# Reciprocals of three blocks repeated by transfers inside SBUF, keys' weight in one load, and a new order of the work

## The chip, the cores and the metric

The kernel runs on one core of a Trainium2 chip. The core has an engine for matrix products (TensorE, PE in the profile; its weight loads are listed apart as PEld), one for elementwise work on 128 lanes (VectorE, DVE), one for activation functions (ScalarE, ACT), one for general work (GpSimd, POOL) and a sequencer that issues transfers (SyncE, SP). Sixteen DMA engines carry these transfers. On-chip memory is SBUF (128 partitions) and PSUM (eight banks of 2 KB in each partition, written by PE and read by DVE and ACT). The engines run side by side, each through its own list of instructions in order, and wait for one another by semaphores.

The metric is the device time of one execution in microseconds (us).

## The reference

One layer over 2048 tokens of width 512, in bfloat16: linear attention with 32 heads of width 16, then a dense block with relu, each behind a layer norm and with a residual.

```python
h  = x + A(layernorm(x), wqkv, wo)
h2 = h + B(layernorm(h), w1, w2)

def A(x, wqkv, wo):
    q, k, v = heads(x @ wqkv)                   # 32 heads of 16
    phi = lambda t: where(t > 0, t + 1, exp(t)) + 1e-6
    pq, pk = phi(q), phi(k)
    kv  = einsum("bhsd,bhse->bhde", pk, v)      # one 16 x 16 matrix a head
    z   = einsum("bhsd->bhd", pk)
    num = einsum("bhqd,bhde->bhqe", pq, kv)
    den = einsum("bhqd,bhd->bhq", pq, z) + 1e-6 # one number a token and head
    return merge(num / den) @ wo

def B(x, w1, w2):                               # w1: 512 x 1792, w2: 1792 x 512
    return relu(x @ w1) @ w2
```

## The kernel before

Tokens are cut into 16 tiles of 128 and into 4 blocks of 512. Everything that is computed is a named step. The text `ORDER` at the head of the file lists the steps, with a tile or block, a part and a PSUM bank as numbers behind the name; a loop at the end of the file calls them one by one, and so fixes the order in which each engine, and SP's queue, meets its own instructions. An instruction that waits holds all that stand behind it on its engine. The blocks are numbered 0 to 3 in the order; "blocks 2 to 4" of the change are those with the numbers 1 to 3.

*Keys.* Loads of the input are `lx` (L212); weights come by `lk`, `lq`, `lv`, `lo`, `l1`, `l2` (L215; `lk.0.2` loads the first two of the four 128-row parts of the keys' weight). Statistics of a tile are `S` and `A` (L229, L230), the reciprocal deviation is `R` (L235, L236), the normalized tile is `N` (L243). Its transpose goes over PE (`T`, L262, evicted by `E` on ACT, L272, or `V` on DVE, L275) or over a transposing transfer on SP (`X`, L283). `K` is the product for the keys (L291); the feature map is `F` and `U` on ACT (L309, L312) and `M` and `D` on DVE (L316, L319). `G` adds each tile's product of normalized input and keys (L343) into four PSUM banks, `za` sums the keys on DVE (L351), `z` finishes the sum (L366). `gA` (ACT, L380) and `gD` (DVE, L383) evict G's banks in two halves, `kv` and `kx` (L388, L396) make the heads' matrices and `m` multiplies them by `wo` (L400), evicted by `mD` (L406) or `mA` (L403).

*Queries.* `Q` is the product for one 128-row part of a block's queries (L299), `qF`, `qU`, `qM`, `qD` its feature map on the same lines as the keys', two parts at once. `d4` forms the denominators of a block (L414), `dl4` and `dx4` take the logarithm and the exponential of its negative on ACT (L420, L425), so that `rd` holds 1/den: 8 heads for each of the four parts, in partitions 32j to 32j+7. To multiply the queries, each of these rows must stand in 16 partitions. For block 0 PE repeats them (`rp`, L430) and DVE multiplies out of PSUM (`rm`, L436). For blocks 1 to 3 `wb` (L442) writes `rd` to DRAM, and eight transfers `rb` (L445) read it back, each into 16 partitions of `rr` and all four parts; `dm` (L452) then multiplies two parts of the block on DVE. There is one `rr` for all blocks.

*Output of the attention and the dense block.* `h` is the product for one tile (L461), `hD` adds the residual on DVE (L467), `s` and `a` are the second statistics (L231, L232), `n` subtracts the mean (L250), `r` the reciprocal deviation; the transposes are `x` (SP, L284) or `t` (PE, L262, evicted by `v` on DVE, L281, or `e` on ACT, L278). `p` is the product with one 128-row part of `w1` for a block (L476), `ph` for half a block (L485); the relu goes out on ACT (`pA`, L491) or DVE (`pD`, L496), two parts at once. `f` is the product with `w2` for a tile, in two halves of seven parts (L505), `fo` scales and adds the residual (L513), `fd` stores (L520). The last tile's `f` is cut into three pieces by columns.

Of the kernel before, what the change touches and what calls it, by code (L numbers as in the profile page):

```python
# [15 lines left out]


ORDER = """
table const masks warm.70.7.64 warm.3.7 lx.1.1 S.1 lx.0.1 S.0 lx.3.1 lx.2.1 lx.4.2 A.1 S.3 A.0 R.1.1 R.0.1 S.2
A.3 N.1 A.2 N.0.0.2 N.0.2.2 S.5 R.2.2 T.0.0.0.2 T.0.3.2.2 T.1.1 warm.1.7 E.0.2.2 E.0.0.2 lk.0.2 lk.2.2 N.3  # L20
T.3.3 A.5 S.4 N.2 A.4 lx.6.2 K.0.0 T.2.2 E.1 K.1.1 R.4.2 V.3 F.0.1 U.0.1 F.1.1 U.1.1 V.2 K.2.2 N.4 T.4.0 F.2.1
E.4 M.0.1 N.5 lx.8.4 D.0.1 S.6 S.7 M.1.1 A.6 A.7 D.1.1 S.8 R.6.2 G.0 T.5.1 K.3.3 K.4.0 E.5 G.1 K.5.1 U.2.1
F.3.1 U.3.1 N.7 S.9 A.8 N.6 M.2.1 A.9 M.3.1 D.2.1 R.8.2 lx.12.4 X.7 X.6 F.4.2 U.4.2 G.2 D.3.1 N.8 S.13 N.9
A.13 M.4.2 S.12 D.4.2 A.12 R.12.2 G.3 K.7.3 K.6.2 X.8 X.9 lq.0.2 F.6.2 U.6.2 G.4 K.8.0 S.11 S.10 A.10 N.13
A.11 M.6.2 N.12 K.9.1 R.10.2 U.8.2 F.8.2 D.6.2 X.13 X.12 S.15 N.10 A.15 S.14 A.14 N.11 M.8.2 D.8.2 R.14.2 N.15
N.14 za.4 X.10 X.11 lq.2.2 X.15 X.14 lv.0.2 l1.2.2 lv.2.2 l2.7.7 lo.0.2 lo.2.2 l1.0.2 G.5 G.6 G.7 K.13.1
K.12.0 G.8 K.10.2 K.11.3 F.12.2 U.12.2 F.10.2 U.10.2 Q.0.0.0 Q.0.1.1 G.9 qU.0.0.2 M.12.2 za.6 M.10.2 D.12.2
D.10.2 za.8 za.10 K.14.2 K.15.3 G.10 G.11 G.12 G.13 F.14.2 U.14.2 qF.0.0.2 Q.0.2.0 M.14.2 za.12 D.14.2 G.14 zf
G.15 zhi zlo qM.0.0.2 qD.0.0.2 z.2.2 z.0.2 z.1.2 Q.0.3.1 z.3.2 zc gA.0.2 Q.1.1.3 Q.1.0.2 gD.2.2 qF.0.2.2
qU.0.2.2 qF.1.0.2 qU.1.0.2 kv.2.4 kv.1.4 kv.3.4 kv.0.4 qM.0.2.2 zh qD.0.2.2 qM.1.0.2 kx qD.1.0.2 Q.1.3.1  # L30
Q.1.2.0 qF.1.2.2 m.2.6 m.3.7 d4.0.3 m.0.4 m.1.5 mD.2.2 mD.0.2 Q.2.0.2 dl4.0 dx4.0 qU.1.2.2 Q.2.1.3 rp.0.3.7
# [7 lines left out]
s.4 a.4 s.7 a.5 n.4 a.7 p.0.13.3 p.0.12.2 r.0.4 pD.0.12.2 pA.0.10.2 d4.2.0.2 dl4.3 dx4.3 f.0.4.0.7 dl4.2 dx4.2
f.1.5.0.7 n.5 n.7 f.3.7.0.7 f.0.4.7.7 f.2.6.7.7 f.1.5.7.7 x.4 x.7 wb.2 x.5 x.6 p.1.1.1 p.1.0.0 rb.2.0 rb.2.4  # L40
rb.2.6 rb.2.1 wb.3 rb.2.5 fo.0 rb.2.7 rb.2.2 rb.2.3 p.1.2.2 p.1.3.3 pD.1.0.2 p.1.5.1 p.1.4.0 pA.1.4.2 r.4.4
pD.1.2.2 fo.2 dm.2.2.2 dm.2.0.2 f.3.7.7.7 p.1.8.0 p.1.6.2 h.10.6 hD.10 fo.1 fd.1 fo.3 rb.3.6 rb.3.2 rb.3.7
p.1.7.3 h.8.4 pA.1.6.2 p.1.9.1 h.11.7 hD.8 f.4.4.0.7 p.1.10.2 hD.11 s.10 s.11 a.11 n.11 pA.1.8.2 p.1.13.1
h.9.5 hD.9 s.9 a.9 f.7.7.0.7 p.1.11.3 a.10 s.8 rb.3.3 rb.3.0 rb.3.4 rb.3.1 rb.3.5 p.1.12.0 pA.1.10.2 pA.1.12.2
f.5.5.0.7 f.7.7.7.7 n.10 n.9 a.8 r.8.4 x.9 fd.2 dm.3.2.2 dm.3.0.2 n.8 fd.3 fd.0 fo.7 x.8 x.10 x.11 f.6.6.0.7
f.5.5.7.7 h.15.7 fo.5 f.6.6.7.7 p.2.0.0 h.13.5 p.2.1.1 f.4.4.7.7 p.2.2.2 fo.6 pA.2.0.2 p.2.4.0 h.14.6 p.2.3.3
pA.2.2.2 hD.15 hD.13 s.15 fo.4 p.2.5.1 h.12.4 p.2.7.3 pA.2.4.2 p.2.6.2 hD.14 s.13 p.2.8.0 p.2.9.1 hD.12 s.14
a.15 a.13 s.12 a.14 a.12 pD.2.6.2 r.12.4 n.15 pA.2.8.2 n.14 n.13 n.12 x.13 fd.7 fd.6 x.15 fd.5 x.14 x.12
f.11.7.0.7 f.10.6.0.7 f.9.5.0.7 p.2.12.0 p.2.11.3 p.2.10.2 p.2.13.1 pD.2.10.2 pA.2.12.2 f.8.4.0.7 f.9.5.7.7
p.3.0.0 p.3.1.1 f.10.6.7.7 pA.3.0.2 p.3.3.3 p.3.5.1 p.3.4.0 p.3.2.2 pA.3.4.2 f.8.4.7.7 p.3.9.1 pD.3.2.2  # L50
p.3.6.2 p.3.8.0 f.11.7.7.7 p.3.7.3 fo.11 pA.3.8.2 fo.9 fd.4 fo.10 fo.8 p.3.12.0 p.3.13.1 pD.3.12.2 fd.10 fd.9
pA.3.6.2 f.13.5.0.7 p.3.11.3 p.3.10.2 pD.3.10.2 f.12.4.0.7 f.15.7.0.14.0.2 f.12.4.7.7 fd.8 fd.11 f.14.6.0.7
f.13.5.7.7 fo.15.0.2 fo.12 fo.13 fd.12 fd.13 fd.15.0.2 f.14.6.7.7 fo.14 fd.14 f.15.5.0.14.3.1 fo.15.3.1
# [5 lines left out]
def kernel(  # L59
# [288 lines left out]
    def op_za(t):  # L350
# [205 lines left out]
```

## Time and profile before

| What | Value |
|---|---|
| Three runs | 170.84, 218.47, 170.45 us; median 170.84 |
| Span of the profiled execution | 169.2 us |
| Its time outside the span | not recorded; the two lower runs lie 1.25 and 1.64 us above the span |
| Busy: DVE, ACT | 101.0 us (60%), 65.4 us (39%) |
| Clock granted to PE | full in all of the 40 slices |
| DVE's wait for PE at the relu eviction (L496) | 26.7 us, in 6 waits |
| ACT's wait for PE at the relu eviction (L491) | 57.4 us, in 13 waits |
| Matmuls of 512 columns | 379 ns each on the page, 216 ns apart in a run of them |

The span runs from the first to the last instruction. The profile's durations of single matmuls overlap; what a run of them costs is read from the chain of waits, which follows the end of the program back, at each step to what released it. Idle time of DVE and ACT is mostly time in which they wait for PE.

### The profile page before, as it was taken

How to read it: one execution, taken by the hardware profiler on the slowest of the kernel's cores; microseconds unless marked ns; L12 is line 12 of the kernel's file. 1: busy time of each engine (PE TensorE's matmuls, PEld its weight loads, DVE VectorE, ACT ScalarE, POOL GpSimd, SP SyncE). 2: the span in 40 equal slices, each digit the busy share in tenths (PEclk: the TensorE clock that was granted, in tenths of full speed). 3: DMA queues.
4: the chain of work that ended last, by engine and by line, in shares of the span. 5: the costliest groups of instructions: out<-in, count | busy, mean ns of one | idle time of the engine just before them, and what ended most of it. 6: DMA issues, size and time to landing. Idle time of an engine off the chain costs nothing.

```text
span 169.2 us, 2376 instructions
## 1 busy us (share of the span) xinstructions
PE 163.5 (97%) x906; PEld 79.9 (47%) x922; DVE 101.0 (60%) x208; ACT 65.4 (39%) x96; POOL 4.7 (3%) x21
## 2 busy tenths in 40 slices
...
GB/s 135 279 210 50 111 119 153 281 364 259 1 2 4 62 133 208 0 4 59 104 147 2 18 94 48 155 62 0 0 0 97 124 31 0 0 0 127 1 31 93
DMA packets 23163, 15.10 MB, mean 89 GB/s; under 512 B 13808, under 2 KB 22128, under 8 KB 23152
## 3 DMA queue, kind: packets, MB, share of 16 engines
...
q8 instruction: 7, 0.11, 0.3%
...
## 4 chain that ended last, share of the span: by engine, by line
PE 91%; DMA 3%; SPq 1%; issue 1%; DVE 1%
PE bk L505 29%; PE bk L476 26%; PE bk L343 8%; PE bk L461 8%; PE bk L291 8%; PE bk L299 7%; DMA wk_sb<-in_A_wqkv_dram 3%; PE bk L485 2%; SPq L212 1%; PE bk L262 1%; DVE pqs L436 1%; PE bk L414 1%; PE bk L400 1%; PE bk L388 1%; PE bk L366 0%
## 5 line engine op out<-in xcount | busy, mean ns | idle before, releaser
L505 PE MATMUL bk<-w_sb,at 128*128 128x512 bf16 (+2 forms) x248 | 50.7, 355 | 0.2
L476 PE MATMUL bk<-lnT,w_sb 128*128 128x512 bf16 x203 | 47.9, 379 | 0.2
L491 ACT ACTIVATE at<-bk 128x1024 bf16<-128x1024 f32 x19 | 19.2, 1023 | 64.7 <-PE bk L476 57.4
L505 PEld LDWEIGHTS <-at 128*128 128x128 bf16 x252 | 23.5, 98 | 25.3 <-issue 0.4
L476 PEld LDWEIGHTS <-w_sb 128*128 128x128 bf16 x208 | 20.4, 98 | 24.3
L496 DVE TENSOR_SCALAR at<-bk 128x1024 bf16<-128x1024 f32 x9 | 11.0, 1219 | 26.7 <-PE bk L476 26.7
L513 DVE SCALAR_TENSOR_TENSOR gT<-bk,rstd,h_nat 128x512 bf16<-128x512 f32 (+2 forms) x18 | 12.1, 689 | 21.6 <-PE bk L505 19.2
L309 ACT ACTIVATE eb<-bk 128x1024 bf16<-128x1024 f32 (+1 forms) x18 | 16.6, 928 | 5.8 <-PE bk L291 4.3
L312 ACT ACTIVATE rb<-bk 128x1024 bf16<-128x1024 f32 (+1 forms) x18 | 16.4, 925 | 2.8 <-PE bk L299 2.4
L467 DVE TENSOR_TENSOR h_nat<-bk,x_nat 128x512 bf16<-128x512 f32 x16 | 10.9, 684 | 9.6 <-PE bk L461 9.5
L461 PE MATMUL bk<-m_sb,pqs 128*128 128x512 bf16 x63 | 15.9, 379 | 0.3 <-DVE pqs L436 0.2
L291 PE MATMUL bk<-wk_sb,lnT 128*128 128x512 bf16 x62 | 15.3, 379 | 0.2 <-DMA wk_sb<-in_A_wqkv_dram 0.2
L299 PE MATMUL bk<-lnT,wq_sb 128*128 128x512 bf16 x62 | 15.2, 379 | 0.1
L343 PE MATMUL bk<-at,h_nat 128*128 128x512 bf16 x55 | 13.2, 379 | 0.1
L229 DVE BATCH_NORM_STATS2 st<-x_nat 128x6 f32<-128x512 bf16 x16 | 10.6, 677 | 1.8 <-DMA x_nat<-in_A_x_dram 1.8
L231 DVE BATCH_NORM_STATS2 st<-h_nat 128x6 f32<-128x512 bf16 x16 | 10.6, 680 | 0.1
L461 PEld LDWEIGHTS <-pqs 128*128 128x128 bf16 x64 | 6.1, 98 | 8.0 <-DVE pqs L436 0.7
L343 PEld LDWEIGHTS <-h_nat 128*128 128x128 bf16 x64 | 6.2, 98 | 7.3
L291 PEld LDWEIGHTS <-lnT 128*128 128x128 bf16 x64 | 6.1, 98 | 7.4 <-issue 0.5
L299 PEld LDWEIGHTS <-wq_sb 128*128 128x128 bf16 x64 | 5.9, 98 | 6.6 <-issue 0.2
L316 DVE TENSOR_SCALAR eb<-eb 128x1024 bf16<-128x1024 bf16 (+1 forms) x18 | 6.8, 386 | 2.1 <-ACT eb L309 2.1
L235 ACT ACTIVATE rstd<-mv,eps 128x2 f32<-128x2 f32 (+2 forms) x13 | 3.8, 295 | 7.0 <-DVE mv L230 4.7
...
## 6 DMA issues: line engine op xcount, KB each, us to landing
...
out_dram<-gT SPq DMA_DIRECT2D x15, 128.0 KB, 1.9
rr<-scr SPq DMA_DIRECT2D x24, 64.0 KB, 2.7
...
x_nat<-in_A_x_dram SPq DMA_DIRECT2D x4, 128.0 KB, 2.2
...
```

The lines of the kernel that those rows point to most:

```text
L291: nc.tensor.matmul(bk[:, b, :], lhsT=lnT[c][:, kd, j * P : (j + 1) * P], rhs=wk_sb[:, kd, :], start=(kd == 0), stop=(kd == KD - 1),)
L299: nc.tensor.matmul(bk[:, b, :], lhsT=wq_sb[:, kd, j * P : (j + 1) * P], rhs=lnT[c][:, kd, :], start=(kd == 0), stop=(kd == KD - 1),)
L309: nc.scalar.activation(out=buf(eb, kind, i, n), in_=bank(at_bank[kind, i], n), func=ACT.Exp)
L312: nc.scalar.activation(out=buf(rb, kind, i, n), in_=bank(at_bank[kind, i], n), func=ACT.Relu)
L343: nc.tensor.matmul(bk[:, KD + kd, :], lhsT=ln_nat[:, t, kd * P : (kd + 1) * P], rhs=pk(t)[:, 0, :], start=(t == 0), stop=(t == NT - 1),)
L461: nc.tensor.matmul(bk[:, b, :], lhsT=pqs[:, (c * KD + jb) % NQ, j * P : (j + 1) * P], rhs=m_sb[:, jb, :], start=(jb == 0), stop=(jb == KD ...
L467: nc.vector.tensor_tensor(out=h_nat[:, t : t + n, :], in0=bank(at_bank["h", t], n), in1=x_nat[:, t : t + n, :], op=ALU.add,)
L476: nc.tensor.matmul(bk[:, b, :], lhsT=w1_sb[:, kd, f * P : (f + 1) * P], rhs=lnT[c][:, kd, :], start=(kd == 0), stop=(kd == KD - 1),)
L491: nc.scalar.activation(out=acts[c % 2][:, f : f + n, :], in_=bank(at_bank["p", c, f], n), func=ACT.Relu)
L496: nc.vector.tensor_scalar(out=acts[c % 2][:, f : f + n, :], in0=bank(at_bank["p", c, f], n), scalar1=0.0, scalar2=None, op0=ALU.max,)
L505: nc.tensor.matmul(bk[:, b, 0 : w * P], lhsT=acts[c % 2][:, f, j * P : (j + 1) * P], rhs=w2_sb[:, f, k * P : (k + w) * P], start=(f == 0), ...
L513: nc.vector.scalar_tensor_tensor(out=o_t[:, t % NO, cols], in0=bk[:, at_bank["f", t, k], 0 : w * P], scalar=rstd2[:, t : t + 1], in1=h_nat ...
```

## The change

The reciprocals of blocks 1 to 3 no longer go to DRAM. Four transfers `rs` for each block read the 8 rows of a part j straight out of `rd` in SBUF, each row 16 times, and write the 128 partitions of `rr[:, j, :]`. The keys' weight comes in one load of 512 KB, the queries' weight in one load of 512 KB ahead of the last loads of the input, and the four `Q` of block 0 stand among the first keys. `gA` becomes a `gD`, one `mD` an `mA`, one `V` an `E`, one `v` an `e`; four of the relu evictions go from ACT to DVE. `n` now gives the mean minus the value, so that the relu evictions multiply by -1. The bookkeeping of `G`, `za` and `z` allows any order of tiles. The whole order is new. The diff, with the order cut to the part around the reciprocals and the start:

```diff
 ORDER = """
-table const masks warm.70.7.64 warm.3.7 lx.1.1 S.1 lx.0.1 S.0 lx.3.1 lx.2.1 lx.4.2 A.1 S.3 A.0 R.1.1 R.0.1 S.2
-A.3 N.1 A.2 N.0.0.2 N.0.2.2 S.5 R.2.2 T.0.0.0.2 T.0.3.2.2 T.1.1 warm.1.7 E.0.2.2 E.0.0.2 lk.0.2 lk.2.2 N.3
...
-rp.0.0.4 rp.0.1.5 rp.0.2.6 Q.2.2.0 Q.2.3.1 qM.1.2.2 rm.0.0.2 rm.0.2.2 h.0.4 qD.1.2.2 hD.0 h.1.5 h.3.7 qU.2.0.2
-qU.2.2.2 qF.2.0.2 qF.2.2.2 d4.1.4 h.2.6 dl4.1 dx4.1 Q.3.2.0 Q.3.3.1 s.0 hD.1 a.0 hD.3 s.1 n.0 a.1 hD.2 n.1 s.3
-s.2 a.3 qU.3.2.2 qF.3.2.2 x.0 wb.1 rb.1.2 rb.1.4 rb.1.6 rb.1.0 rb.1.7 rb.1.5 rb.1.3 rb.1.1 l2.0.7 a.2 n.3
-Q.3.1.3 t.1.5 Q.3.0.2 n.2 v.1 t.3.7 t.2.6 v.3 v.2 ph.0.3.1.0 ph.0.2.0.0 ph.0.3.1.1 ph.0.2.0.1 qF.3.0.2
-qU.3.0.2 pA.0.2.2 ph.0.0.2.1 ph.0.0.2.0 ph.0.1.3.1 ph.0.1.3.0 p.0.6.0 p.0.7.1 pD.0.6.2 dm.1.0.2 dm.1.2.2
-qM.2.2.2 qM.2.0.2 pA.0.0.2 p.0.5.3 p.0.4.2 p.0.11.1 p.0.10.0 h.6.6 qM.3.0.2 pA.0.4.2 hD.6 h.4.4 h.5.5 p.0.9.3
...
+table const masks warm.70.7.64 warm.2.7 lx.0.1 S.0 lx.1.1 S.1 A.0 R.0.1 A.1 lx.3.1 lx.2.1 R.1.1 S.3 N.0.0.2 A.3
+R.3.1 T.0.1.0.2 N.0.2.2 T.0.3.2.2 E.0.0.2 N.1 T.1.1 N.3 E.0.2.2 S.2 lk.0.4 A.2 T.3.4 V.3 lx.4.2 E.1 K.0.5 K.1.2
+R.2.1 N.2 U.0.1 F.0.1 lx.6.2 T.2.7 E.2 K.3.1 S.4 S.5 A.4 M.0.1 F.1.1 K.2.4 A.5 S.7 lq.0.4 M.1.1 R.4.2 Q.0.1.3
+A.7 lx.12.4 F.3.1 N.4 N.5 M.3.1 S.6 D.0.1 lv.2.2 A.6 U.1.1 U.3.1 D.3.1 T.4.7 lx.8.4 lo.2.2 T.5.5 E.4 E.5 Q.0.2.0
+R.6.2 K.4.6 lv.0.2 K.5.7 Q.0.3.1 D.1.1 S.15 N.6 A.15 F.2.1 U.2.1 Q.0.0.2 F.4.2 S.13 N.7 A.13 U.4.2 S.9 S.14 A.9
+qF.0.0.2 qU.0.0.2 M.2.1 A.14 S.8 D.2.1 A.8 S.12 R.8.2 G.1 G.0 G.3 M.4.2 A.12 X.7 N.9 R.14.2 R.12.2 N.8 D.4.2
+N.13 X.6 X.9 S.10 S.11 qF.0.2.2 K.7.3 A.10 qM.0.2.2 K.6.2 G.4 G.2 G.5 F.6.2 U.6.2 A.11 R.10.2 N.12 N.14 qM.0.0.2
...
+K.14.2 F.14.2 U.14.2 M.14.2 G.8 zf D.14.2 G.11 G.10 G.13 zhi zlo qM.1.0.2 qD.1.0.2 G.15 z.2.2 G.14 G.12 gD.0.2
+gD.2.2 z.3.2 z.1.2 z.0.2 Q.1.3.1 Q.1.2.0 qF.1.2.2 kv.3.3 kv.2.3 kv.0.3 kv.1.3 zc zh d4.0.4 kx Q.2.0.2 m.2.5
+m.3.6 qU.1.2.2 qM.1.2.2 qD.1.2.2 m.1.1 dl4.0 m.0.0 dx4.0 mD.2.2 Q.2.1.3 rp.0.3.7 rp.0.0.4 mA.0.2 rp.0.2.6
+rp.0.1.5 Q.2.2.0 qU.2.0.2 qF.2.0.2 Q.2.3.1 qU.2.2.2 rm.0.0.2 rm.0.2.2 d4.1.5 qM.2.0.2 h.0.3 hD.0 s.0 h.1.4 dl4.1
+dx4.1 hD.1 rs.1.0 h.2.2 qF.2.2.2 Q.3.0.3 Q.3.1.4 h.3.0 Q.3.2.5 a.0 hD.2 n.0 s.1 s.2 a.1 qU.3.0.2 qF.3.0.2 a.2
+n.1 hD.3 x.0 rs.1.2 rs.1.3 t.1.2 e.1 n.2 rs.1.1 Q.3.3.6 s.3 a.3 qM.3.0.2 n.3 t.2.7 v.2 ph.0.2.0.0 ph.0.0.2.0
+t.3.4 l2.0.7 r.0.4 qM.2.2.2 ph.0.1.3.0 ph.0.3.1.0 v.3 ph.0.0.2.1 ph.0.1.3.1 ph.0.3.1.1 dm.1.2.2 qF.3.2.2
+ph.0.2.0.1 qU.3.2.2 pA.0.0.2 qM.3.2.2 dm.1.0.2 h.7.7 h.6.2 p.0.6.6 qD.2.2.2 qD.2.0.2 qD.3.0.2 qD.3.2.2 hD.7
+pD.0.2.2 hD.6 s.7 d4.2.4.2 dl4.2 s.6 dl4.3 h.5.3 p.0.7.7 a.7 pD.0.6.2 hD.5 a.6 dx4.2 p.0.10.0 h.4.2 hD.4 n.7
+rs.2.2 rs.2.1 rs.2.3 s.5 p.0.11.1 s.4 a.5 rs.2.0 dx4.3 n.6 p.0.9.5 p.0.4.6 p.0.5.7 x.7 p.0.13.3 p.0.8.4 p.0.12.2
+a.4 r.4.4 n.5 dm.2.0.2 n.4 pD.0.4.2 f.1.6.0.7 pD.0.10.2 dm.2.2.2 h.9.0 h.8.1 pD.0.8.2 h.11.5 x.5 pD.0.12.2 x.4
+rs.3.0 rs.3.1 dm.3.0.2 hD.8 f.1.6.7.7 hD.9 s.8 hD.11 a.8 h.10.7 s.9 x.6 p.1.7.2 p.1.6.1 rs.3.2 rs.3.3 dm.3.2.2
+a.9 hD.10 s.11 p.1.11.5 s.10 n.9 a.10 a.11 n.8 n.10 h.14.0 pA.1.6.2 h.12.2 n.11 hD.14 x.11 r.8.4 h.13.7 hD.12
...
+f.8.7.0.7 fo.14 fo.11 fd.11 fo.13 fd.13 fd.14 f.8.7.7.7 fo.8 fd.8 f.15.0.0.14.2.1 fo.15.2.1 fd.15.2.1
 """
...
     def op_n(t):
         nc.vector.tensor_scalar(
-            out=hn[:, t % NQ, :], in0=h_nat[:, t, :], scalar1=mv2[:, t, 0:1], scalar2=None,
-            op0=ALU.subtract,
+            out=hn[:, t % NQ, :], in0=h_nat[:, t, :], scalar1=-1.0, scalar2=mv2[:, t, 0:1],
+            op0=ALU.mult, op1=ALU.add,
         )
...
+    def op_rs(c, j):
+        rows = rd[j * Q4 : j * Q4 + P // DH, c, :]
+        nc.sync.dma_start(
+            out=rr[:, j, :], in_=rows.rearrange("h (o n) -> h o n", o=1).broadcast_to([P // DH, DH, CW])
+        )
...
     def op_pA(c, f, n):
         nc.scalar.activation(
-            out=acts[c % 2][:, f : f + n, :], in_=bank(at_bank["p", c, f], n), func=ACT.Relu
+            out=acts[c % 2][:, f : f + n, :], in_=bank(at_bank["p", c, f], n), func=ACT.Relu, scale=-1.0
         )
 
     def op_pD(c, f, n):
         nc.vector.tensor_scalar(
             out=acts[c % 2][:, f : f + n, :], in0=bank(at_bank["p", c, f], n),
-            scalar1=0.0, scalar2=None, op0=ALU.max,
+            scalar1=-1.0, scalar2=0.0, op0=ALU.mult, op1=ALU.max,
         )
```

More of the change, by code (lines that the diff above doesn't have):

```diff
@@ L24 @@
[L24 to L28, printed above, removed]
@@ L29 @@
-G.15 zhi zlo qM.0.0.2 qD.0.0.2 z.2.2 z.0.2 z.1.2 Q.0.3.1 z.3.2 zc gA.0.2 Q.1.1.3 Q.1.0.2 gD.2.2 qF.0.2.2
-qU.0.2.2 qF.1.0.2 qU.1.0.2 kv.2.4 kv.1.4 kv.3.4 kv.0.4 qM.0.2.2 zh qD.0.2.2 qM.1.0.2 kx qD.1.0.2 Q.1.3.1
-Q.1.2.0 qF.1.2.2 m.2.6 m.3.7 d4.0.3 m.0.4 m.1.5 mD.2.2 mD.0.2 Q.2.0.2 dl4.0 dx4.0 qU.1.2.2 Q.2.1.3 rp.0.3.7
-rp.0.0.4 rp.0.1.5 rp.0.2.6 Q.2.2.0 Q.2.3.1 qM.1.2.2 rm.0.0.2 rm.0.2.2 h.0.4 qD.1.2.2 hD.0 h.1.5 h.3.7 qU.2.0.2
-qU.2.2.2 qF.2.0.2 qF.2.2.2 d4.1.4 h.2.6 dl4.1 dx4.1 Q.3.2.0 Q.3.3.1 s.0 hD.1 a.0 hD.3 s.1 n.0 a.1 hD.2 n.1 s.3
@@ L34 @@
-s.2 a.3 qU.3.2.2 qF.3.2.2 x.0 wb.1 rb.1.2 rb.1.4 rb.1.6 rb.1.0 rb.1.7 rb.1.5 rb.1.3 rb.1.1 l2.0.7 a.2 n.3
-Q.3.1.3 t.1.5 Q.3.0.2 n.2 v.1 t.3.7 t.2.6 v.3 v.2 ph.0.3.1.0 ph.0.2.0.0 ph.0.3.1.1 ph.0.2.0.1 qF.3.0.2
-qU.3.0.2 pA.0.2.2 ph.0.0.2.1 ph.0.0.2.0 ph.0.1.3.1 ph.0.1.3.0 p.0.6.0 p.0.7.1 pD.0.6.2 dm.1.0.2 dm.1.2.2
-qM.2.2.2 qM.2.0.2 pA.0.0.2 p.0.5.3 p.0.4.2 p.0.11.1 p.0.10.0 h.6.6 qM.3.0.2 pA.0.4.2 hD.6 h.4.4 h.5.5 p.0.9.3
-h.7.7 p.0.8.2 pA.0.8.2 f.2.6.0.7 qD.3.0.2 qD.2.2.2 hD.5 qM.3.2.2 hD.4 s.6 qD.2.0.2 qD.3.2.2 a.6 n.6 hD.7 s.5
@@ L39 @@
[L39 to L53, printed above, removed]
@@ L54 @@
-fd.15.3.1 f.15.4.0.14.2.1 fo.15.2.1 fd.15.2.1
+table const masks warm.70.7.64 warm.2.7 lx.0.1 S.0 lx.1.1 S.1 A.0 R.0.1 A.1 lx.3.1 lx.2.1 R.1.1 S.3 N.0.0.2 A.3
[3 more added lines that the diff above has]
+R.6.2 K.4.6 lv.0.2 K.5.7 Q.0.3.1 D.1.1 S.15 N.6 A.15 F.2.1 U.2.1 Q.0.0.2 F.4.2 S.13 N.7 A.13 U.4.2 S.9 S.14 A.9
@@ new lines @@
+qF.0.0.2 qU.0.0.2 M.2.1 A.14 S.8 D.2.1 A.8 S.12 R.8.2 G.1 G.0 G.3 M.4.2 A.12 X.7 N.9 R.14.2 R.12.2 N.8 D.4.2
+N.13 X.6 X.9 S.10 S.11 qF.0.2.2 K.7.3 A.10 qM.0.2.2 K.6.2 G.4 G.2 G.5 F.6.2 U.6.2 A.11 R.10.2 N.12 N.14 qM.0.0.2
+K.9.3 N.11 M.6.2 qU.0.2.2 qD.0.0.2 D.6.2 N.15 X.8 K.8.2 X.13 K.13.1 X.12 F.8.2 U.8.2 G.6 N.10 K.12.0 F.12.2
+qD.0.2.2 M.8.2 X.11 K.11.3 za.4.1 X.10 D.8.2 za.6.0 M.12.2 G.7 U.12.2 za.8.0 K.10.2 F.10.2 M.10.2 X.15 X.14
+D.12.2 Q.1.1.1 U.10.2 D.10.2 lo.0.2 Q.1.0.0 qU.1.0.2 qF.1.0.2 l1.0.2 l1.2.2 za.10.0 za.12.0 G.9 l2.7.7 K.15.3
@@ new lines @@
+a.4 r.4.4 n.5 dm.2.0.2 n.4 pD.0.4.2 f.1.6.0.7 pD.0.10.2 dm.2.2.2 h.9.0 h.8.1 pD.0.8.2 h.11.5 x.5 pD.0.12.2 x.4
+rs.3.0 rs.3.1 dm.3.0.2 hD.8 f.1.6.7.7 hD.9 s.8 hD.11 a.8 h.10.7 s.9 x.6 p.1.7.2 p.1.6.1 rs.3.2 rs.3.3 dm.3.2.2
+a.9 hD.10 s.11 p.1.11.5 s.10 n.9 a.10 a.11 n.8 n.10 h.14.0 pA.1.6.2 h.12.2 n.11 hD.14 x.11 r.8.4 h.13.7 hD.12
+s.14 p.1.10.4 hD.13 h.15.3 a.14 s.12 x.9 p.1.2.1 x.8 pA.1.10.2 n.14 p.1.3.2 a.12 hD.15 s.13 n.12 a.13 s.15 x.12
+p.1.12.4 p.1.13.5 f.2.0.0.7 p.1.5.7 a.15 pA.1.2.2 r.12.4 n.13 n.15 fo.1 x.10 p.1.4.6 f.3.1.0.7 pA.1.12.2 p.2.0.2
@@ new lines @@
+pA.1.4.2 p.2.1.3 f.0.5.0.7 p.2.3.7 p.2.2.6 f.2.0.7.7 fo.2 pA.2.0.2 f.3.1.7.7 p.2.9.3 fo.3 p.2.8.2 pA.2.2.2
+f.0.5.7.7 fo.0 fd.2 pA.2.8.2 p.1.0.4 p.2.13.3 p.2.12.2 pA.2.12.2 p.2.11.7 p.2.10.6 x.15 p.1.1.5 pA.2.10.2
+pD.1.0.2 p.2.6.2 x.13 p.2.7.3 pD.2.6.2 p.1.8.4 p.1.9.5 x.14 pD.1.8.2 f.6.0.0.7 f.6.0.7.7 fo.6 f.4.7.0.7 fd.0
+f.4.7.7.7 fd.1 fo.4 f.5.3.0.7 fd.3 fd.4 fd.6 f.5.3.7.7 f.7.0.0.7 fo.5 f.7.0.7.7 fo.7 fd.7 p.3.8.6 p.3.9.7
+p.3.7.4 p.3.6.3 pA.3.8.2 p.3.0.6 p.3.1.7 pA.3.6.2 p.3.4.2 p.3.5.3 pA.3.0.2 pD.3.4.2 p.3.11.5 p.3.10.4 p.3.2.1
@@ L55 @@
+p.3.3.2 pD.3.10.2 p.3.13.7 p.3.12.6 pD.3.2.2 pA.3.12.2 f.15.5.0.14.0.2 fo.15.0.2 f.15.3.0.14.3.1 fo.15.3.1
+p.2.5.5 p.2.4.4 f.12.2.0.7 fd.5 fd.15.3.1 pD.2.4.2 f.12.2.7.7 fo.12 f.9.3.0.7 f.9.3.7.7 fo.9 f.10.5.0.7
+f.10.5.7.7 fo.10 f.14.0.0.7 f.14.0.7.7 f.11.5.0.7 f.11.5.7.7 f.13.1.0.7 fd.15.0.2 fd.10 fd.9 fd.12 f.13.1.7.7
+f.8.7.0.7 fo.14 fo.11 fd.11 fo.13 fd.13 fd.14 f.8.7.7.7 fo.8 fd.8 f.15.0.0.14.2.1 fo.15.2.1 fd.15.2.1
 """
@@ L87 @@
     NO = 4
-    ZT = 12
     const = ctx.enter_context(tc.tile_pool(name="const", bufs=1))
```

19 lines of the change are left out of this document (12 added, 7 removed).

## The prediction

> **What bounds the kernel now.** I read the page first. TensorE (PE) is busy for 163.5 of 169.2 us at a full granted clock, and the chain that ended last is 91% PE:
>
> ```profile
> span 169.2 us, 2376 instructions
> ...
> PE 163.5 (97%) x906; PEld 79.9 (47%) x922; DVE 101.0 (60%) x208; ACT 65.4 (39%) x96; POOL 4.7 (3%) x21
> ...
> PE 91%; DMA 3%; SPq 1%; issue 1%; DVE 1%
> ```
>
> Then the chain in order of time, to see where PE is not the bound:
>
> ```profile
> 3.61 4.93 DMA wk_sb<-in_A_wqkv_dram
> 8.54 0.04 issue
> 8.58 0.59 PE bk L291 x2
> ...
> 9.39 1.73 PE bk L291 x8
> ...
> 49.68 1.23 DVE pqs L436
> ...
> 58.70 3.49 PE bk L485 x32
> ...
> 75.80 0.55 PE bk L414 x8
> ```
>
> From 8.58 us to 166.53 us PE runs almost without a gap; the only other piece of note is the 1.2 us on VectorE (DVE) at 49.68. The matmul work of the new order is the same (only eight warm-up matmuls go). So a gain can come only from the 8.5 us ahead of the dense stretch, some 2.7 us behind it, and that one wait; a loss comes from every wait that the new order puts in front of PE. PE's prices are read here: four 512-column matmuls 0.86 us (eight in 1.73), four of 256 columns 0.44 (32 in 3.49), eight L414 0.55.
>
> **The reciprocals.** Twenty-four reads of 64 KB and three writes to DRAM go, twelve transfers of 128 KB come. The groups of DMA issues give the old prices, the timeline of the DMA queue (SP) when they ran:
>
> ```profile
> rr<-scr SPq DMA_DIRECT2D x24, 64.0 KB, 2.7
> ...
> scr<-rd SPq DMA_DIRECT2D x3, 128.0 KB, 1.9
> ```
>
> ```profile
> 56.56 0.53 SPq L442 DMA_DIRECT2D scr<-rd  x1
> 58.48 3.62 SPq L445 DMA_DIRECT2D rr<-scr  x8
> ```
>
> What goes saves nothing: asked for the tile `rr`, the trace names nobody who waited for it. DVE reached the multiply (L452) at 65.17 us, after the last issue at 61.7 had landed. SP loses about 5 us of issues (27 of 0.3 to 0.5 us for 12), and SP is not on the chain.
>
> What comes has no row: a transfer out of 8 partitions of `rd`, each read 16 times, into 128. Let r be the time for which one of them holds the queue. Below, the bound is SP's own pace, 0.42 us an issue (the median of L445). Above, the nearest row is the old `rr` transfer, the only one with few partitions (16, on the writing side). While eight of them ran, the windows show:
>
> ```profile
> 60.00:61.00 1.00, 1.00 (x12) 0.89 (x10) 0.00 (x0) 0.75 (x2) 0.00 (x0) 1.00 0.43 137
> ...
> 62.00:63.00 1.00, 0.95 (x6) 0.51 (x6) 0.00 (x0) 0.77 (x1) 0.00 (x0) 1.00 0.53 148
> ...
> 65.00:66.00 1.00, 1.00 (x7) 0.47 (x5) 1.00 (x3) 0.31 (x1) 0.00 (x0) 1.00 1.08 385
> ```
>
> The last column is GB/s: 137 for 16 partitions, 385 for a weight load over 128. At 137/16 = 8.6 GB/s a partition, 8 partitions carry 68 GB/s, and 128 KB take 1.9 us. I take 1.9, the nearest row in partitions touched, though those reads may have been held by the pace of issue. From issue to the first packet is 1.05 us (the first load: issued 0.80, first packet 1.83); from the last packet to landing 0.4 (`scr`: 58.06 to 58.46).
>
> **Block 2** (reciprocals index 1). Let T be the start of h.0. PE then has h.0, h.1, h.2, Q.3.0, Q.3.1, h.3, Q.3.2, Q.3.3 (8 x 0.86), three transposes (0.66) and eight half projections (8 x 0.44): h.7 is due at T+11.1. It needs all four parts of `rr` through dm.1.2 and dm.1.0. On DVE one start follows the last by 0.61 (L467), 0.60 (L231, L319, L452), 0.09 (L232), 0.27 (L250), 0.33 (L316), 1.14 (L496). n.0 is done at T+3.75 (h.2 ends at 2.6, 0.2 to its add, 0.61, 0.27), dm.1.2 can start at 9.1, dm.1.0 at 10.2. On SP the transfers rs.1.2, rs.1.3 and rs.1.1 stand behind x.0, a transposing load that holds SP for 1.2 us (L284, x1 1.19) from T+3.8; they issue from 5.05. First packets at 6.1, last landing 6.1 + 3r + 0.4 = T+12.2. dm.1.0 is done at 12.8, h.7 starts at 12.95: **+1.85**. Behind the waiting multiply on DVE stand four L319 and the adds to the residual, and PE waits for it in turn.
>
> **Block 3** (index 2). Let U be the start of h.7. d4.2 ends at U+3.1; Ln 0.69 twice and Exp 0.63 on ScalarE (ACT) put the first rs.2 at U+5.05. Four in a row land at 6.1 + 4r + 0.4 = U+14.1. The last issued, rs.2.0, belongs to dm.2.0, which DVE reaches at U+10.8 (from U-0.2: four L319, four L467, four L231, four L232, three L250, two L496, 10.7 together, and 0.3 of gaps). DVE stands for **3.3 us**, with n.4 and four relu evictions behind it; f.1.6.0, due at U+12.6, needs pD.0.4 among these, so PE stands too: the new order leaves it no other work.
>
> **Block 4** (index 3). rs.3.0 waits for dm.2.0 (one buffer `rr`, free at 14.7) and stands behind x.4 on SP (n.4 at 15.0, 1.2 of issue): issued at 16.2, rs.3.1 lands at 16.2 + 1.05 + 3.8 + 0.4 = U+21.45, against dm.3.0's turn at 16.8 + 3.3 = 20.1 (10.8, two L452, L250, four L496: 6.0): 1.35 late. rs.3.2 and rs.3.3, behind them and x.6 (0.5 of data), land at 25.7, 0.5 after dm.3.2's turn; dm.3.2 ends at 26.3 and h.14, due at 21.7 + 3.3 = 25.0, is late by **1.4**. The threshold at which the waits begin is r = 1.07 (6.5 + 4r = 10.8).
>
> **The start.** `lk.0.4` comes fifth on SP, ahead of lx.4. In the trace the second half of `wk` landed at 8.54, 1.65 us after the 1.31 MB ahead of it had moved (134 GB/s over 0 to 4 us, 267 over 4 to 8: 6.9). Now 1.05 MB are ahead: 5.9 + 1.65 = 7.6. Before, two of K.0's matmuls (0.43) were done by 8.54; now T.3 (0.22) is done sooner: 8.54 - 7.6 - 0.43 + 0.22 = 0.75 us earlier. The first queries need `wq` at about 11.3 and its 512 KB land, at the same rates, at 11.6: 0.3 back. Four Q (3.5 us of PE) come ahead of K.4, which covers DVE's wait for lx.8 (now behind `wq` and half of `wv`, due 16.6 against DVE's turn at 15.6). Net **-0.5**, bounds -1.0 (no wait for `wq`) and +0.5 (the transposes X.7, X.6 behind 3.9 MB of loads instead of 2.6 come 1 us late).
>
> **Off the path**, at nothing: the other eviction engine for gT and m (a DVE copy 1.21 against 1.02 on ACT, under Q.1.3 and Q.1.2, 1.7 us); two operations in L250 and L496 instead of one (L243 with two runs 397 ns on 128x512, L250 344: at most 0.05 each, DVE is 60% busy; without cover, in block 3, 0.3); the sign in the relu eviction, an immediate. At the end a full store stands ahead of the last small one on SP, 0.5 us of issue beside 0.8 us of matmuls: 0.
>
> **The sum:** -0.5 + 1.85 + 3.3 + 1.4 = +6.05 us; span 169.2 to 175.3. The two runs that agree, 170.45 and 170.84, lie 1.25 and 1.6 us above the span; on the median: **176.9 us**.
>
> **Rivals.** *The transfers are quick enough* (0.33): for it speaks `scr<-rd`, the same tile and 128 KB, which lands in 1.9 us; at the pace of issue the last rs.2 lands at U+8.5, ahead of 10.8. It holds for any r under 1.07. Then no wait is left but 0.3 inside block 3: the start alone counts, 170.84 - 0.5 = 170.3. [...] *DVE frays* (0.07): block 1's relu evictions go to DVE six times of seven and leave less than 0.5 us of slack at f.1.6, h.9 and h.11; 0.3 to 1 us at each of three places with quick transfers: 171.5 to 173.5. That the change does not do what it says has no room: the order is written out by hand.
>
> **How the numbers follow.** My forecast has 0.35: few partitions cost, but not more than the nearest row says. The range runs from the quick case with the start at its best (170.84 - 1.0 = 169.8) to the near side of the two paths, 184, for r of 2.6. Slower by over 2% (above 174.3 us) takes the forecast but for r under 1.6, and the two paths: 0.6. Within 2%, about what a measurement of this kernel can tell from no change: the quick transfers, most of the fraying and the low end of the forecast: 0.38. Faster by over 2% would need 3.4 us of a start and an end that hold at most 1.5: 0.02.
>
> **What would show it.** In the profile after: transfers into `rr` with a landing near 3.4 us for one and 9 us for the last of four; a wait of DVE for `rr` at the multiply, 1 to 3 us per block, where there was none; PE's idle time ahead of L461 and L505; K.0's first matmul at 7.6 us. The prediction is wrong if `rr` has no waiter (then 170.3), or if the landings of four exceed 11 us (then 182 and more).

## The result and the profile after

The changed kernel took **186.22 us** (185.59 to 186.34, four runs), the one before 170.88 beside it: a ratio of 1.0906, 95% interval 1.0884 to 1.0929. The execution of before that took 218.47 us is left out of the ratio. It is 15.3 us slower, and lies 2.2 us above the upper end of the predicted range. The profiled execution took 186.34 us with a span of 184.6, which is 15.4 more than the span before.

The page of the changed kernel, the lines that answer to those shown of before (and the row of granted clocks):

```profile
span 184.6 us, 2357 instructions
...
PE 167.3 (91%) x903; PEld 80.9 (44%) x920; DVE 104.6 (57%) x210; ACT 62.4 (34%) x96; POOL 4.8 (3%) x21
...
PEclk9999999999999958996999999999999999999999
...
PE 66%; DMA 14%; DVE 8%; SPq 6%; ACT 2%; issue 2%; DVEq 0%
```

PE's share of the chain fell from 91% to 66%, and transfers, DVE and SP's queue hold 28%. And two dents stand in the clock row, which was full before. The chain in order of time says which transfers:

```profile
56.67 8.08 DMA rr<-rd
...
65.99 3.19 PE bk L472 x7
...
76.37 6.29 DMA rr<-rd
...
91.80 6.46 DMA rr<-rd
```

All are transfers into `rr`, one group for each block, and the first of them releases (through DVE) the matmuls of h.7. The waits of the changed kernel, in us in total, times, and the longest:

```profile
DVE pqs L463 <- DMA rr<-rd: 15.6, 5, 4.9
...
PE bk L472 <- DVE pqs L463: 7.3, 2, 5.0
...
PE bk L516 <- DVE at L507: 3.9, 1, 3.9
```

Nobody waited for `rr` before. Now DVE does for 15.6 us, and PE behind it. PE's timeline (start, length of the run of matmuls, and in brackets the idle time ahead of it and what ended it) places these waits:

```profile
6.95 1.89 PE L295 MATMUL bk<-wk_sb,lnT 128*128 128x512 bf16 x8
...
65.99 3.19 PE L472 MATMUL bk<-m_sb,pqs 128*128 128x512 bf16 x7 [4.99 <-DVE pqs L463]
...
84.89 3.13 PE L516 MATMUL bk<-w_sb,at 128*128 128x512 bf16 x7 [3.85 <-DVE at L507]
...
95.36 1.02 PE L487 MATMUL bk<-lnT,w_sb 128*128 128x512 bf16 x4 [0.59 <-DVE h_nat L478]
...
99.10 2.33 PE L472 MATMUL bk<-m_sb,pqs 128*128 128x512 bf16 x10 [2.29 <-DVE pqs L463]
```

These are h.7, f.1.6, one product with `w1` and h.14. The first line is K.0, the first product for the keys. The bracket at h.7 is 0.4 us too long, because the record of its first matmul is missing from the trace: the page has one matmul less than weight loads for `h`, and DVE's timeline has the multiply that h.7 waits for:

```profile
L472 PE MATMUL bk<-m_sb,pqs 128*128 128x512 bf16 x63 | 16.8, 408 | 7.3 <-DVE pqs L463 7.3
...
L472 PEld LDWEIGHTS <-pqs 128*128 128x128 bf16 x64 | 6.4, 104 | 16.2 <-DVE pqs L463 7.6
```

```profile
64.84 0.69 DVE L463 TENSOR_TENSOR pqs<-pqT,rr 128x1024 bf16<-128x1024 bf16 x1 [1.25 <-DMA rr<-rd]
```

The multiply ends at 65.53, the first weight load of h.7 is at 65.59, and there h.7 starts; its wait is 4.6 us. (In the experiments, rows of x7 at h.7 and h.6, which are eight, lack the first one too; at full clock their bracket is 0.2 us too long.) So the brackets come to 4.6 + 3.85 + 0.59 + 2.29 = **11.3 us** of waits. Then the matmuls themselves: the seven of f.1.6 hold PE for 3.13 us, where 1.67 is what they take in the fastest kernel below. The windows show why (busy time of PE, PEld, DVE, ACT, POOL, then granted clock, DMA share, GB/s):

```profile
58.00:60.00 2.00, 2.00 (x23) 1.82 (x21) 0.67 (x2) 1.41 (x2) 0.00 (x0) 1.00 0.43 50
60.00:62.00 2.00, 1.00 (x10) 0.65 (x7) 0.00 (x0) 1.02 (x1) 0.00 (x0) 1.00 0.46 53
62.00:64.00 2.00, 0.00 (x0) 0.00 (x0) 1.03 (x2) 0.00 (x0) 0.00 (x0) 1.00 0.86 193
...
66.00:68.00 2.00, 2.00 (x5) 0.75 (x5) 2.00 (x5) 0.00 (x0) 0.00 (x0) 0.50 0.30 106
68.00:70.00 2.00, 2.00 (x6) 0.76 (x5) 2.00 (x3) 0.00 (x0) 0.00 (x0) 0.50 0.00 0
...
72.00:74.00 2.00, 2.00 (x11) 0.91 (x10) 0.69 (x1) 1.58 (x3) 0.00 (x0) 1.00 0.00 0
```

Two readings. **The transfers:** while only they run (58 to 61 us) some 50 GB/s flow. In the trace's packet records a packet of theirs, 1,024 bytes, takes 140 ns, and some 24 of them finish in each half microsecond; 128 KB so take 2.67 us. **The clock:** in the trace's record it was 0.5 from 63.99 to 70.82 us and from 84.47 to 87.89, each time from within a long wait to some way behind it. In 66 to 70 us PE gets 11 matmuls done, in 72 to 74 eleven in half the time. The twelve matmuls of h.7, h.6 and p.0.6 take 5.2 us (65.59 to 70.82) for 2.7 at full clock (66.11 to 68.79 in the run with a filled wait, below), the seven of f.1.6 (without the modelled end of the last) 2.9 for 1.5: **3.9 us**.

The balance is cleanest against the same order of work with quick transfers (the first experiment, a span of 168.7 us), whose trace has the same 930 weight loads. Load by load, the changed kernel starts 0.3 us ahead of it, then falls back by 5.0, 4.0, 0.8 and 2.7 us at the four waits and by 3.9 us at half clock: -0.3 + 12.4 + 3.9 = 16.0, the difference of the two spans. The waits cost 12.4 and not the 11.3 of the brackets, in part because a bracket begins at the modelled end of the matmul ahead, which lies 0.16 us (379 less 216 ns) behind the moment at which the next one could have started.

SP's queue for eight of the twelve issues (start, length, times); behind the first four stands the load of `w2`:

```profile
51.72 0.81 SPq L457 DMA_DIRECT2D rr<-rd  x1
...
55.17 3.49 SPq L457 DMA_DIRECT2D rr<-rd  x3
58.70 2.51 SPq L213 DMA_DIRECT2D w_sb<-in_B_w_dram  x1
73.08 5.50 SPq L457 DMA_DIRECT2D rr<-rd  x4
```

### The profile page after: what moved, and what is told of

Read it like the earlier page. It is cut to its first block, busy times and chain, and to the rows that moved or that the text cites. A ratio compares the mean times of both kernels' runs of the same rounds, so it can differ in the third digit from the quotient of the medians.

```text
span 184.6 us, 2357 instructions
## 1 busy us (share of the span) xinstructions
PE 167.3 (91%) x903; PEld 80.9 (44%) x920; DVE 104.6 (57%) x210; ACT 62.4 (34%) x96; POOL 4.8 (3%) x21
## 4 chain that ended last, share of the span: by engine, by line
PE 66%; DMA 14%; DVE 8%; SPq 6%; ACT 2%; issue 2%; DVEq 0%
PE bk L516 24%; PE bk L487 19%; DMA rr<-rd 11%; PE bk L347 6%; PE bk L472 5%; PE bk L303 5%; PE bk L295 4%; DVE st L227 4%; SPq L457 3%; SPq L288 2%; DMA lnT<-h_nat 2%; DVE h_nat L241 1%; DMA x_nat<-in_A_x_dram 1%; DVE pqs L463 1%; ACT ld L425 1%
## 5 line engine op out<-in xcount | busy, mean ns | idle before, releaser
L524 DVE SCALAR_TENSOR_TENSOR gT<-bk,rstd,h_nat 128x512 bf16<-128x512 f32 (+2 forms) x18 | 12.4, 692 | 38.9 <-PE bk L516 38.0
L502 ACT ACTIVATE at<-bk 128x1024 bf16<-128x1024 f32 x15 | 15.3, 1023 | 56.5 <-PE bk L487 48.8
L507 DVE TENSOR_SCALAR at<-bk 128x1024 bf16<-128x1024 f32 x13 | 15.7, 1220 | 15.7 <-PE bk L487 15.7
L472 PE MATMUL bk<-m_sb,pqs 128*128 128x512 bf16 x63 | 16.8, 408 | 7.3 <-DVE pqs L463 7.3
L303 PE MATMUL bk<-lnT,wq_sb 128*128 128x512 bf16 x62 | 15.4, 379 | 0.1
L463 DVE TENSOR_TENSOR pqs<-pqT,rr 128x1024 bf16<-128x1024 bf16 x6 | 4.1, 690 | 15.6 <-DMA rr<-rd 15.6
```

The source lines that it names most:

```text
L303: nc.tensor.matmul(bk[:, b, :], lhsT=wq_sb[:, kd, j * P : (j + 1) * P], rhs=lnT[c][:, kd, :], start=(kd == 0), stop=(kd == KD - 1),)
L472: nc.tensor.matmul(bk[:, b, :], lhsT=pqs[:, (c * KD + jb) % NQ, j * P : (j + 1) * P], rhs=m_sb[:, jb, :], start=(jb == 0), stop=(jb == KD ...
L502: nc.scalar.activation(out=acts[c % 2][:, f : f + n, :], in_=bank(at_bank["p", c, f], n), func=ACT.Relu, scale=-1.0)
L507: nc.vector.tensor_scalar(out=acts[c % 2][:, f : f + n, :], in0=bank(at_bank["p", c, f], n), scalar1=-1.0, scalar2=0.0, op0=ALU.mult, op1= ...
L524: nc.vector.scalar_tensor_tensor(out=o_t[:, t % NO, cols], in0=bk[:, at_bank["f", t, k], 0 : w * P], scalar=rstd2[:, t : t + 1], in1=h_nat ...
```

## The experiments

The theory, A in the expectations: what such a transfer moves goes with where its source rows stand in SBUF, and eight of them in neighbouring partitions made the 49 GB/s. Rivals: the form of the transfer itself (eight source rows, each repeated 16 times, and from 58 to 61 us never more than eight packets at once) is slow from any source; the new order, not the transfers, leaves no room; the half clock, not the waits, is the larger part.

### Heads four partitions apart

The same twelve transfers and the same order, but the eight heads of a part stand in partitions 32j, 32j+4, ... 32j+28 of `rd` in place of 32j to 32j+7. The masks that place them (for `zhd`, and for block 0's `rp`) change with it; the amount of work does not. If the theory holds, packets of 1,024 bytes go from 140 ns to some 46, as out of DRAM before, and the time to 170.3 us (169.8 to 171.5).

```diff
-        keep(mask_h[:], mask_h[:], [[0, KD], [-DH, Q4]], 0, 1)
-        keep(mask_h[:], mask_h[:], [[0, KD], [DH, Q4]], DH - 1, -1)
+        m4 = mask_h.rearrange("p k (a b) -> p k a b", b=4)
+        nh = Q4 // 4
+        keep(m4, m4, [[0, KD], [-DH, nh], [-1000, 4]], 0, 1)
+        keep(m4, m4, [[0, KD], [DH, nh], [0, 4]], DH - 1, -1)
...
-        rows = rd[j * Q4 : j * Q4 + P // DH, c, :]
+        rows = rd[j * Q4 : j * Q4 + 4 * (P // DH) : 4, c, :]
```

> The new order and the same twelve transfers, but the eight heads of a part stand four partitions apart in `rd` (32j, 32j+4, ..., 32j+28) instead of side by side; the masks that place them are changed to match. [...] Theory B (the form: 8 source rows are split over few transfer engines) and theory C (one row read 16 times is slow, wherever it stands): the packets stay near 140 ns and the time near 186 us.

Measured: **170.10 us** (169.94 to 170.91, ten runs), ratio to before 0.9959 [0.9943, 0.9975]. A packet takes 46 ns, a transfer is through in 0.70 to 0.75 us, and the transfers alone move 172 to 197 GB/s in the half microseconds that they fill. From the page and, for the tile `rr`, the issues (shortest, median and longest ns, first and last start):

```profile
span 168.7 us, 2357 instructions
...
PEclk9999999999999999999999999999999999999999
```

```profile
L460 SPq DMA_DIRECT2D rr<-rd x12: 607/607/807, 52.1 to 77.1; - x12
```

```profile
66.01 2.71 SPq L460 DMA_DIRECT2D rr<-rd  x4
```

The last line, from SP's timeline, is block index 2: four issues in 2.7 us instead of 5.5. Nobody waits for `rr`, no wait of PE is left at h.7, f.1.6 or h.14, and the clock is full throughout. The partitions of the source are the cause of the whole loss, with the waits and the clock as its two ways of acting; and this is the fastest version found, 0.4% under the kernel before.

### Heads two partitions apart

`b=2` for `b=4`, with steps of 2. If the rate goes with the distance of the rows, twice the 49 GB/s were expected, packets of some 70 ns and 170.3 to 172 us.

> The new order and transfers with the heads of a part two partitions apart (32j, 32j+2, ..., 32j+14), the masks to match. [...] If any gap between the rows is enough (a conflict between direct neighbours), packets are back at 46 ns and the rate at 190 GB/s as with four partitions between them: 170.1 us.

Measured: 171.25 us (one run). Packets of some 74 ns, 98 to 109 GB/s, 1.3 us a transfer. PE's timeline has two small waits left:

```profile
61.65 1.67 PE L475 MATMUL bk<-m_sb,pqs 128*128 128x512 bf16 x7 [0.53 <-DVE pqs L466]
...
74.60 1.67 PE L519 MATMUL bk<-w_sb,at 128*128 128x512 bf16 x7 [0.27 <-DVE at L510]
```

Side by side, two apart, four apart: 49, 102 and some 190 GB/s, at 140, 74 and 46 ns a packet. The second doubling falls short of 2. My estimate for this, from the packets: at 46 ns for 1,024 bytes an engine carries 22 GB/s, and eight carry some 178, near to what was measured; packets out of DRAM take 46 ns as well (next run). That eight engines are at work is read from the slow case: from 58 to 61 us never more than eight data packets run at once, and the data of a transfer end with eight packets of 4 bytes.

### The same four transfers, out of DRAM

`rd` is written to DRAM once, and four transfers of the same form read it back.

```diff
-        rows = rd[j * Q4 : j * Q4 + P // DH, c, :]
+        rows = scr[c][j, 0 : P // DH, :, :]
...
-dx4.1 hD.1 rs.1.0
+dx4.1 hD.1 wb.1 rs.1.0
-rs.2.2 rs.2.1 rs.2.3
+wb.2 rs.2.2 rs.2.1 rs.2.3
-rs.2.0 dx4.3 n.6
+rs.2.0 dx4.3 wb.3 n.6
```

> The new order; each block's reciprocals are written to DRAM in one transfer at the place of the first of its four, and the same four transfers (8 rows, each 16 times, into 128 partitions) read from DRAM instead of SBUF. Theory A (few paths into SBUF on the reading side): packets of about 46 ns, the four transfers of a block issue-bound at 0.6 to 0.7 us each; the write in front adds 1.9 us to the way, so dm.2.0 waits 0.3 to 1 us: 170.5 to 172 us. Theory B (the form over few engines): packets stay near 140 ns and the time is at least that of the changed kernel, 186 to 189 us. Theory C (repeated rows of SBUF) agrees with A here.

Measured: 174.23 us (one run), slower than expected. Its packets take 46 ns, a transfer 0.8 to 0.9 us (some 150 to 170 GB/s): the form and the eight engines are quick from another source, and that rival falls. What the time missed is on SP and PE:

```profile
51.60 0.34 SPq L447 DMA_DIRECT2D scr<-rd  x1
55.13 0.75 SPq L457 DMA_DIRECT2D rr<-scr  x1
55.99 1.22 SPq L288 DMA_TRANSPOSE lnT<-hn  x1
```

```profile
58.86 1.03 PE L494 MATMUL bk<-lnT,w_sb 128*128 128x256 bf16 x8 [1.79 <-DMA lnT<-hn]
...
77.57 1.67 PE L514 MATMUL bk<-w_sb,at 128*128 128x512 bf16 x7 [1.71 <-DVE at L505]
```

The first read waits on SP for the write to land, and the transposing load x.0 stands behind it: it goes out at 55.99, where after the change it went at 53.73. PE waits 1.79 us for its result, and 1.71 more at f.1.6. The write's way through DRAM has a cost in this order that I had not put into the expectation.

### The new order with the old way through DRAM

`wb` and the 24 `rb` in the places of `rs`, all else of the change kept, but that the last block's eight reads stand in one go ahead of dm.3.0, and x.6 ahead of them:

```diff
-dx4.1 hD.1 rs.1.0 h.2.2
+dx4.1 hD.1 wb.1 h.2.2
-n.1 hD.3 x.0 rs.1.2 rs.1.3 t.1.2 e.1 n.2 rs.1.1
+n.1 hD.3 x.0 rb.1.2 rb.1.4 rb.1.6 rb.1.0 rb.1.7 rb.1.5 t.1.2 e.1 n.2 rb.1.3 rb.1.1
...
```

> The new order with the reciprocals on the old way: one write to DRAM and eight reads of 64 KB per block, in the places of the new transfers (the last block's reads in one go ahead of dm.3.0, with x.6 moved ahead of them). It tells what the order costs by itself when the way is the old one. By my count of queue time (eight issues of 0.42 us behind a write of 1.9 us) h.7 comes 0.9 us late, dm.2.0 2 us and dm.3.0 some 3 us: 173 to 177 us under every theory of the slow transfer; 170.3 us if the old way keeps up.

Measured: 182.78 us (one run), 6 us above the upper end. DVE waits 8.4 us in two waits for `rr`, and PE behind it:

```profile
65.41 2.79 PE L472 MATMUL bk<-m_sb,pqs 128*128 128x512 bf16 x7 [3.23 <-DVE pqs L463]
...
82.18 2.49 PE L516 MATMUL bk<-w_sb,at 128*128 128x512 bf16 x7 [2.39 <-DVE at L507]
```

The new order asks for the reciprocals sooner than either slow way gives them. And the clock is at half behind both waits, 3.41 us each time, though the waits are short.

### The old order with the slow transfers

The kernel before, with each `wb` removed and each pair of `rb` replaced by one `rs` (parts 0, 2, 1, 3).

> The order of before, with the writes and reads over DRAM replaced by the four transfers inside SBUF in their places: this part of the change alone. If a transfer holds the queue for 2.67 us as measured in the changed kernel (49 GB/s), the four of block 1 issued from 56.5 us land at 68.7 us, against dm.1.0's turn at 65.2 and h.6's at 67.2: a wait of about 3 us and a spell of half clock after it; blocks 2 and 3 have over 8 us of room and wait 0 to 1 us: 174 to 177 us. If the order is what makes the transfers late and not their rate, nothing waits: 170.5 to 171 us.

Measured: **170.94 us** (one run), nothing lost; expected were 174 to 177. From the waits, the windows and SP's timeline:

```profile
DVE pqs L457 <- DMA rr<-rd: 2.4, 3, 1.3
```

```profile
62.00:64.00 2.00, 1.95 (x10) 0.90 (x10) 0.08 (x1) 1.02 (x1) 0.00 (x0) 1.00 0.42 97
```

```profile
56.45 5.69 SPq L451 DMA_DIRECT2D rr<-rd  x4
```

The packets of the first transfer are as slow (140 ns), and DVE waits for 2.4 us, but PE does not wait for it: the old order reaches the multiplies later. So neither the slow transfers nor the new order is the cost by itself; it is a new order with no slack over transfers that need it. The four were also quicker than four times 2.67 (10.7 us): some 8 us from the first packet to the last (7.9 for block index 2), at 49 GB/s for the first and up to 97 behind it.

### The old order with the quick transfers

The same with the heads four apart.

> The order of before with the transfers inside SBUF and the heads four partitions apart: the fast transfer alone, without the new order. Nobody waited for `rr` before, so a faster way is worth nothing: 170.7 us (170.3 to 171.1). The difference to the new order with the same transfers (170.1) is then what the new order is worth by itself, 0.5 to 0.7 us at the start. If the fast transfers and not the order brought that, this kernel is at 170.1 as well.

Measured: 171.07 us (170.78 to 171.72, ten runs), ratio 1.0017 [1.0001, 1.0033]. Quick reciprocals are worth nothing to the old order. Against 170.10 with the same transfers, the new order is worth 1.0 us; the transfers only allow it.

### Matmuls in place of the first wait

In the changed kernel, 23 matmuls whose result nobody reads fill the wait ahead of h.7, so that PE is not idle there.

```diff
-dm.1.0.2 h.7.7 h.6.2
+dm.1.0.2 warm.23.7 h.7.7 h.6.2
```

> The changed kernel with 23 matmuls of 512 columns put in front of h.7, into a bank that is free there and whose result nobody reads. They take 23 x 0.216 = 4.97 us, the wait of 4.99 us that TensorE has there. If the granted clock falls because TensorE stood idle, the 12 matmuls behind the wait run 0.216 us apart instead of 0.41, nothing else moves, and 2.4 us come back: 183.8 us (183.3 to 184.5). If the half clock has another cause, the time stays at 186.2 us or grows.

Measured: 185.05 us (184.36 to 185.92, four runs), ratio 1.0838 [1.0789, 1.0887]. In the median about half of what was expected came back. PE's timeline, from the slowest of the four executions:

```profile
66.11 1.89 PE L472 MATMUL bk<-m_sb,pqs 128*128 128x512 bf16 x8
...
82.89 3.14 PE L516 MATMUL bk<-w_sb,at 128*128 128x512 bf16 x7 [3.88 <-DVE at L507]
...
97.17 3.46 PE L472 MATMUL bk<-m_sb,pqs 128*128 128x512 bf16 x10 [2.12 <-DVE pqs L463]
```

h.7 and h.6 run at full clock now. The matmuls of d4.2 behind them begin at 68.79 us where they began at 70.82, so 2.0 us came back there, although the fill holds h.7 until 66.11 (it started at 65.59): the idle time was the cause of the half clock there, as expected. But the spell at f.1.6 doubled (81.15 to 87.98), and a third came at h.14: its ten matmuls take 3.46 us instead of 2.33. The change had no half clock at h.14, after a wait of 2.29 us. The four executions differ in this: 185.92 us at a mean granted clock of 0.970, 185.64 at 0.981, 184.46 at 0.988 and 184.36 at 0.991. By these clocks they spent some 11, 7, 4.4 and 3.3 us at half, and the two with the least lie inside the expected range.

### The halves of SBUF in another order

Block index 2 issues its parts as 2, 1, 3, 0, and in the packet records its rate rises from 49 to over 100 GB/s by 79 us; block index 1 issues 2, 3, 1 and stays at 49. Parts 0 and 1 stand in the lower 64 partitions, 2 and 3 in the upper. This run swaps the two patterns.

```diff
-rs.1.2 rs.1.3 t.1.2 e.1 n.2 rs.1.1
+rs.1.2 rs.1.1 t.1.2 e.1 n.2 rs.1.3
-rs.2.2 rs.2.1 rs.2.3 s.5
+rs.2.2 rs.2.3 rs.2.1 s.5
```

> The changed kernel with two transfers swapped in two blocks: block index 1 issues parts 2, 1, 3 (halves of SBUF alternate) where it issued 2, 3, 1; block index 2 issues 2, 3, 1, 0 (halves side by side) where it issued 2, 1, 3, 0. In the old order of work, alternating transfers moved 49 GB/s for the first and some 100 for those behind it, so 2.67 us for the first and about 1.6 for each next. If transfers out of different halves overlap: index 1 needs some 5.9 us instead of 8.0, and PE's wait at h.7 falls from 4.99 to 2.5 to 3.5 us; index 2 takes 1 to 2.7 us longer than 6.3 and the wait at f.1.6 grows from 3.85 to between 5 and 6.5. If the speeding up comes only from a filled queue, whatever the half, both waits stay within 0.5 us of what they were. The total is not what is asked; since one wait falls and one grows it should stay within 3 us of 186.2, with the half clock falling as it may.

Measured: 189.92 us (one run). From the windows and PE's timeline:

```profile
60.00:62.00 2.00, 0.96 (x9) 0.61 (x7) 0.00 (x0) 1.02 (x1) 0.00 (x0) 1.00 0.47 99
...
76.00:78.00 2.00, 2.00 (x11) 0.90 (x10) 1.47 (x6) 0.50 (x2) 0.00 (x0) 1.00 0.44 50
```

```profile
65.16 3.60 PE L472 MATMUL bk<-m_sb,pqs 128*128 128x512 bf16 x8 [4.21 <-DVE pqs L463]
...
86.90 3.15 PE L516 MATMUL bk<-w_sb,at 128*128 128x512 bf16 x7 [6.29 <-DVE at L507]
...
101.16 3.99 PE L472 MATMUL bk<-m_sb,pqs 128*128 128x512 bf16 x10 [2.28 <-DVE pqs L463]
```

The rates changed places: 99 GB/s in 60 to 62 us where there were 53, and 50 in 76 to 78 where there were 58 and then 78. The wait at f.1.6 grew to 6.29 us, as expected. So here transfers out of different halves overlapped, and out of one half they did not. The wait at h.7 fell only from 4.6 to 4.21, not to 2.5 to 3.5. The last landing came 1.4 us sooner (63.39 for 64.75), but it is now part 3, so that both multiplies of the block (0.6 each) come behind it instead of one. The whole is 3.7 us slower, beyond the 3 allowed for: 2.4 at f.1.6, less 0.4 at h.7, and a half clock at h.14 (3.99 us for 2.33, +1.7) that the change had not.

## Why the prediction was wrong, and where it was right

**Right: what bounds the kernel, and what the removed part saves.** PE was the bound, a loss could come only from new waits in front of it, and the 24 reads and three writes saved nothing: without them the old order takes 170.94 and 171.07 us.

**Right in sign, and half the size: the start.** K.0 began at 6.95 us (7.6 was predicted) and h.0 at 49.66, 0.5 earlier than before. That this is the -0.5 of the sum is luck, because PE has not done the same work by then. The new order has d4.1 behind it at h.0 (four matmuls, 0.33 us), and it is free of the wait for DVE inside the first twelve matmuls of `h` (2.60 us for 3.05), the one that the prediction had named as a possible gain and left out of the sum. At equal work, behind the sixteen matmuls of block 0's `h`, d4.1 and eight matmuls of Q.3, the changed kernel is 1.3 us ahead (54.85 for 56.15). With quick transfers in both orders it is 1.1 (55.17 for 56.23), which is the 1.0 us that the new order is worth. Two warm-up matmuls went and not eight; nothing in the sum hung on it.

**Right: the places.** h.7, the multiply of part 0 that holds f.1.6, and h.14 are where PE waits, in that order. The due time of h.7 (T+11.1, with T = 49.66 for the start of h.0) came at T+11.3. The fourth wait, 0.59 us for a residual add, was not foreseen. The costs off the path stayed at nothing: with quick transfers the whole rest of the change gains 1.0 us.

**Wrong: the size of r.** The step is "at 137/16 = 8.6 GB/s a partition, 8 partitions carry 68 GB/s": r was 2.67 us, not 1.9. The row came from transfers that wrote 16 partitions and were held by the pace of issue, as the text itself feared: eight issues of 64 KB in 3.62 us are 145 GB/s, the rate of the row. And the rate goes not by the number of partitions but by where they stand: the spread heads touch eight partitions as well and move some 190 GB/s. Put into the prediction's own steps, 2.67 gives h.7 an extra 4.2 us (measured 4.6; the landing was T+15.1 for a worked-out 14.5, with the load of `w2` moving beside it from some 61.5 us on).

**Wrong: nothing in the sum for the clock.** The prediction priced a wait at its length. At the two long ones the clock was at half for 6.83 and 3.41 us, which cost **3.9 us** in all, and this pushed on what comes next: the first `rs` of block index 2 was issued at U+7.5, not U+5.05 (U, the start of h.7, is 65.59). The chain shown of before has one wait of 1.2 us and a full clock, so no row there gave this price. Which waits half a clock followed is taken up in the last section.

**With r as measured, the steps come near the time, by two errors that cancel.** With 2.67 us for r they hold h.7 by 4.2 us, f.1.6 by 6.4 and h.14 by 4.5, which with the -0.5 of the start makes 185.4 us for a measured 186.22. They have no clock, and they count the four transfers of block index 2 in a row: 6.4 us at f.1.6, where halves that alternate made it 3.85. With the halves side by side it was 6.29. At h.14 the wait was 2.29.

**The two paths of the range and of the 0.6.** No run shows how many paths eight rows of SBUF have. What the runs showed is the rate: 49 GB/s with the rows side by side, 2.67 us a transfer, where the range ends at an r of 2.6; 102 and some 190 with them two and four apart.

**The rival of quick transfers** named a threshold (r of 1.07 us) that fits: with heads four apart r is 0.7 us, no wait is left, and 170.10 stands for the 170.3 that it gave; with heads two apart r is 1.3, and two small waits are left. DVE did not fray.

**The range** went up to r = 2.6 without the clock; with 3.9 us on top of its upper end it would have held the time.
